# Attention and two MoE layers on one core: the last tokens' Q and K loaded with two heads exchanged in half of the batches

## The chip, the cores and the metric

The kernel runs on one core of a Trainium2 chip. A core has five engines that run their own instruction lists side by side: TensorE (PE) for matrix products, VectorE (DVE), ScalarE (ACT) and GpSimd (POOL) for elementwise work, and SyncE (SP), which here issues nearly all DMA transfers. They wait for each other and for landed transfers through semaphores. The metric is the device time of one execution in microseconds (us); lower is better.

## The reference, cut to what matters

Inputs are q, k and v of 8 batches, 8 heads, 576 tokens and 64 columns. Attention is within chunks of 64 tokens, so there are 9 chunks in each batch and head. Its output, read as 4608 tokens by 512 columns, goes through two feed-forward layers:

```python
scores = scale * np.matmul(q_c, k_c.transpose(0, 1, 2, 4, 3))   # per chunk of 64 tokens
attn = softmax(scores); out = np.matmul(attn, v_c)
x = out.transpose(0, 2, 1, 3).reshape(4608, 512)
y = (sigmoid(x @ w_gate) * (x @ w_val)) @ w_out                 # d_ff 1536
h = y @ w_in                                                    # d_ff 2048
g = np.where(h >= 1, h, np.where(h <= -1, 0, (h + 1)**2 / 4))
result = g @ w_out2
```

Weights come as 64-bit floats and all arithmetic is single precision.

## The kernel before, in words

**Stages.** The first, up to about 610 us, holds attention and the first layer's two projections; the rest of the span holds the other products, done by a seven-product (Strassen-like) scheme. Each full-precision product is three passes of rounded operands (lines 528 to 530 of `three`). PE is meant to be busy all through.

**Blocks.** The 4608 tokens are worked in nine blocks of 512. Eight are the first 512 tokens of one batch each. The block in the middle, number 4 (`REST`), collects the last 64 tokens of all eight batches: chunk c of that block is batch c. Each block has four pairs of heads (p = 0 to 3), with the two heads' 64 columns stacked on 128 partitions. While the projections of block b run (12 gate and 12 value columns of weights, 24 slots), the attention of a following block is done in between, one pair every six slots.

**One pair of heads.** `load` brings q and k (line 283 for block 4, line 312 for most others); a letter in `how` says in which layout, and "V", the default and block 4's, is transposed in 32 by 32 squares on DVE (line 336). `s` makes the scores: 16 products of 64 by 64 per pair (line 361; the trace counts two passes of each, x32). `m`, `e`, `n` and `w` make the softmax, `p` transposes the result on PE, `o` multiplies by v (line 422), `x` and `l` split the output into the projection's operands.

**Which part of PE a score product uses.** Its rows are the partitions its operands stand on (0 to 63 or 64 to 127), its columns the partitions it writes. Without exchange, head 0 always reads and writes the lower half and head 1 the upper. With `swap`, the second half of a block's tokens (u = 1) is loaded with the two heads' rows exchanged, so that there head 0 reads the upper partitions and writes the lower, and head 1 the reverse. `swap` holds for layouts V and S in every block but block 4.

**Order of the work.** The code is written out slot by slot: `at(slot, prio, ...)` sorts what is emitted between two projections, and each engine runs its instructions in that order. For blocks 3 and later, pair p of block b starts at slot 24(b-1)+6p-11. Its q is loaded two pairs earlier, its k one slot after that, its v 6.5 slots after its start, and `o` follows at 14. SP's one queue also carries, between these loads, the stores of finished projections (`gT<-sg`, line 845, four `sg` buffers), the raw weights of later layers (`raw`, lines 112 and 116) and the stores of their split forms (`swo`, `swi`, line 192). The program uses eight DMA semaphores in turn, so each issue also waits for the transfer eight places ahead of it.

Of the kernel before, what the change touches and what calls it, by code (L numbers as in the profile page):

```python
# [33 lines left out]
def kernel(  # L34
# [15 lines left out]
    nc = tc.nc  # L50
    P = 128
    B, H, S, D = q.shape
# [5 lines left out]
    BS = 512  # L58
# [176 lines left out]
    REST = NB // 2  # L235
    RS = S - BS

    def batch(blk):
        return blk - (blk > REST)
# [5 lines left out]
    class Whole:  # L245
# [14 lines left out]

        def swap(self, p):

            return self.b != REST and self.how[p] in "VS"

        def load(self, p, which=(0, 1)):
            t = self.alloc("qk") if 0 in which else self.raw[p]
            self.raw[p] = t
            how = self.how[p]
            if how == "V":

                t = t.rearrange("p i (t r) -> p i t r", r=32)
            elif how in "TS":

                t = t.rearrange("p i (j h d) -> p i j h d", h=2, d=D)
            else:
                t = t.rearrange("p i (h j d) -> p i h j d", h=2, d=D)
            for i in which:
                src = (q, k)[i]
                if self.b == REST:
                    for g in range(4):  # L280
                        h, j = divmod(g, 2)
                        for c in range(RS // 32):
                            nc.sync.dma_start(
                                out=t[32 * g:32 * g + 32, i, c::RS // 32],
                                in_=src[:, 2 * p + h, BS + 32 * c:BS + 32 * c + 32, 32 * j:32 * j + 32].rearrange(
                                    "b i r -> i b r"
                                ),
                            )
                else:
                    rows = src[batch(self.b), 2 * p:2 * p + 2, :BS]  # L290
                    if how == "M":
                        nc.sync.dma_start(
                            out=t[:, i].rearrange("i h j d -> i h (j d)"),
                            in_=rows.rearrange("h (i j) d -> i h (j d)", j=NC),
                        )
                    elif how in "TS":
                        n = 2 if self.swap(p) else 1
                        for u in range(n):
                            js = slice(u * NC // n, (u + 1) * NC // n)
                            for h in range(2):  # L300
                                nc.sync.dma_start(
                                    out=t[:, i, js, h],
                                    in_=rows[h ^ u].rearrange("(j i) d -> i j d", i=P)[:, js],
                                )
                    else:
                        n = 2 if self.swap(p) else 1
                        step = BS // n
                        for u in range(n):
                            for g in range(4):
                                h, j = divmod(g, 2)  # L310
                                part = rows[h ^ u, u * step:(u + 1) * step, 32 * j:32 * j + 32]
                                nc.sync.dma_start(
                                    out=t[32 * g:32 * g + 32, i, u * step // 32:(u + 1) * step // 32],
                                    in_=part.rearrange("(t i) r -> i t r", i=32),
                                )
            self.qk[p] = t
# [670 lines left out]
```

## Time and profile before

| | |
|---|---|
| median of 3 runs | 1638.9 us (1638.7 to 1639.31) |
| profiled execution | 1639.61 us, span 1637.8 us |
| PE busy | 1620.7 us, 99% of the span |
| DVE, ACT, POOL busy | 1081.2, 806.7, 360.0 us |
| DMA | 336.31 MB in 375733 packets, q1 busy 63.8% of 16 engines |
| issues on SP of q and k in layout V | 32 KB each |

The profile shows one execution. An engine's line number is that of the kernel; SPq is SP's sequencer, whose issue of a DMA has a duration of its own, and a transfer lands some us after its issue. The chain of waits follows the work that ended last back to the start; a line there says how long the end of the program hung on that piece.

### The profile page before, as it was taken

To read this page: it belongs to the slowest core of one execution; us is meant where nothing else is said; L and a number is where in the kernel's file an instruction comes from. 1 tells how busy PE (TensorE), PEld (TensorE's weight loads), DVE (VectorE), ACT (ScalarE), POOL (GpSimd) and SP (SyncE) were. 2 spreads that over 40 slices of the span, in tenths; PEclk is the share of its full clock that TensorE was granted. 3 is DMA by queue.
4 is the path that set the end of the run, shared out by engine and by line. 5 is a ranking of instruction groups with operands and counts; after the bars stand their busy time and mean duration, and the time that the engine had idled before them with its cause. 6 is when DMAs were issued, how large, how long until landed. Compare 5 with 4: busy or idle time off the path is not lost.

```text
span 1637.8 us, 27009 instructions
## 1 busy us (share of the span) xinstructions
PE 1620.7 (99%) x9764; PEld 1355.9 (83%) x9764; DVE 1081.2 (66%) x1944; ACT 806.7 (49%) x1374; POOL 360.0 (22%) x342
## 2 busy tenths in 40 slices
PE   7999999999999999999999999999999999999998
PEld 6777888888888888888988888889888888888888
DVE  6965554455455521488687766676766887878787
ACT  5764544455545431355455455445443545454544
POOL 2423444344444420000000164240420300000000
PEclk9999999999999999999999999999999999999999
DMA  8957877777778848352636744758659856445252
GB/s 205 269 131 193 236 230 207 206 211 237 223 224 231 264 159 322 138 170 89 218 125 236 269 181 177 289 222 312 237 221 402 337 173 174 140 118 187 71 144 37
DMA packets 375733, 336.31 MB, mean 205 GB/s; under 512 B 260432, under 2 KB 281936, under 8 KB 375600
## 3 DMA queue, kind: packets, MB, share of 16 engines
q1 hardware_dynamic: 375408, 334.39, 63.8%
q8 instruction: 77, 1.26, 0.3%
q14 instruction: 56, 0.46, 0.1%
q0 software_dynamic: 192, 0.20, 0.1%
HBM read 209.19 MB, written 125.30 MB: 204 GB/s over the span
## 4 chain that ended last, share of the span: by engine, by line
PE 95%; DVE 2%; DMA 1%; ACT 1%; SPq 1%; issue 0%; POOL 0%; POOLq 0%; DVEq 0%; ACTq 0%
PE P L528 19%; PE P L530 19%; PE P L529 19%; PE pr L528 11%; PE pr L530 11%; PE pr L529 11%; PE O L422 1%; PE S L361 1%; PE S L404 1%; DMA raw<-in_moe_w_gate_dram 1%; DMA gT<-sg 0%; DVE raw L135 0%; PE PT L404 0%; DMA qk<-in_q_dram 0%; DVE raw L127 0%
## 5 line engine op out<-in xcount | busy, mean ns | idle before, releaser
L528 PE MATMUL P<-op,w 128*128 128x512 f32 (+1 forms) x1540 | 567.3, 368 | 0.5 <-ACT R L616 0.5
L529 PE MATMUL P<-op,w 128*128 128x512 f32 (+1 forms) x1540 | 566.8, 368 | 0.0
L530 PE MATMUL P<-op,w 128*128 128x512 f32 (+1 forms) x1540 | 566.7, 368 | 0.0
L528 PE MATMUL pr<-x,w 128*128 128x512 f32 x864 | 341.7, 395 | 0.0
L530 PE MATMUL pr<-x,w 128*128 128x512 f32 x864 | 336.9, 390 | 0.0
L529 PE MATMUL pr<-x,w 128*128 128x512 f32 x864 | 336.6, 390 | 0.0
L528 PEld LDWEIGHTS P<-op,w 128*128 128x128 f32 x1540 | 290.5, 189 | 49.4 <-ACT R L616 1.3
L529 PEld LDWEIGHTS P<-op,w 128*128 128x128 f32 x1540 | 290.5, 189 | 48.0
L530 PEld LDWEIGHTS P<-op,w 128*128 128x128 f32 x1540 | 290.5, 189 | 47.9
L947 DVE TENSOR_TENSOR sg<-pr,sg 128x512 f32<-128x512 f32 x108 | 74.5, 690 | 300.2 <-PE pr L530 183.0
L595 ACT ACTIVATE op<-u 128x512 fp32r<-128x512 f32 (+1 forms) x280 | 158.7, 586 | 160.1 <-PE P L530 85.7
L618 DVE TENSOR_TENSOR R<-P,R 128x512 f32<-128x512 f32 (+1 forms) x180 | 114.5, 636 | 136.8 <-PE P L530 136.2
L601 DVE TENSOR_TENSOR op<-u,op 128x512 fp32r<-128x512 f32 (+1 forms) x272 | 168.4, 629 | 48.4 <-ACT op L595 45.5
L530 PEld LDWEIGHTS pr<-x,w 128*128 128x128 f32 x864 | 162.2, 188 | 34.4
L528 PEld LDWEIGHTS pr<-x,w 128*128 128x128 f32 x864 | 162.3, 188 | 33.1
L529 PEld LDWEIGHTS pr<-x,w 128*128 128x128 f32 x864 | 162.4, 188 | 32.1
L601 POOL TENSOR_TENSOR op<-y,op 128x512 fp32r<-128x512 f32 (+1 forms) x56 | 66.7, 1205 | 495.2 <-DMA w<-swi 334.5
L944 ACT ACTIVATE sg<-pr 128x512 f32<-128x512 f32 x108 | 64.4, 596 | 199.3 <-PE pr L530 197.5
L595 ACT ACTIVATE op<-in 128x512 fp32r<-128x512 f32 (+1 forms) x210 | 116.5, 585 | 91.9 <-DVE in L591 55.7
L747 ACT ACTIVATE ua<-ua,half 128x1024 f32<-128x1024 f32 (+1 forms) x80 | 82.9, 1060 | 132.2 <-DVE ua L726 131.6
L601 DVE TENSOR_TENSOR op<-in,op 128x512 fp32r<-128x512 f32 (+1 forms) x210 | 128.0, 637 | 22.8 <-ACT op L595 22.4
L616 ACT ACTIVATE R<-P 128x512 f32<-128x512 f32 (+1 forms) x198 | 105.3, 549 | 49.8 <-PE P L530 49.3
(69 smaller groups left out, 1452.4 us busy)
## 6 DMA issues: line engine op xcount, KB each, us to landing
w<-swi SPq DMA_DIRECT2D x84, 512.0 KB, 5.0
uT<-ua SPq DMA_DIRECT2D x64, 512.0 KB, 3.8
u<-uT SPq DMA_DIRECT2D x64, 512.0 KB, 6.2
gT<-sg SPq DMA_DIRECT2D x96, 256.0 KB, 3.9
in<-gT SPq DMA_DIRECT2D x48, 512.0 KB, 5.4
raw<-in_moe_w_out_dram SPq DMA_DIRECT2D x28, 512.0 KB, 5.5
w<-swp SPq DMA_DIRECT2D x28, 512.0 KB, 8.5
swi<-st SPq DMA_DIRECT2D x24, 512.0 KB, 3.9
```

The lines of the kernel that those rows point to most:

```text
L361: nc.tensor.matmul(banks[h ^ u][hs, c], lhsT=t[rows, 0, ts], rhs=t[rows, 1, ts], start=True, stop=True)
L404: nc.tensor.transpose(place, self.SP[p][0][:, c * P:(c + 1) * P], kv_["ident"])
L528: nc.tensor.matmul(o, lhsT=ah, rhs=bh, start=first, stop=False, skip_group_check=open_)
L529: nc.tensor.matmul(o, lhsT=ah, rhs=bl, start=False, stop=False, skip_group_check=open_)
L530: nc.tensor.matmul(o, lhsT=al, rhs=bh, start=False, stop=stop and last, skip_group_check=open_)
L595: nc.scalar.activation(o[:, 0], op_src(p, key), AF.Copy)
L601: eng.tensor_tensor(out=o[:, 1], in0=op_src(p, key), in1=f32(o[:, 0]), op=ALU.subtract)
L616: nc.scalar.activation(r(i), b, AF.Copy)
L618: nc.vector.tensor_tensor(out=r(i), in0=b, in1=r(i), op=ALU.add)
L747: nc.scalar.activation(u, u, AF.Square, scale=0.5, bias=half)
L944: nc.scalar.activation(sg, go, AF.Sigmoid)
L947: nc.vector.tensor_tensor(out=sg, in0=vo, in1=sg, op=ALU.mult)
```

## The change

`swap` now holds for block 4 too, and the loads of that block are cut in two: batches 0 to 3 (u = 0) come as before, batches 4 to 7 (u = 1) with the two heads' rows exchanged. For each of q and k and each pair, eight DMAs of 32 by 8 by 32 elements become sixteen of 32 by 4 by 32, with the same bytes in all. In `s`, which is not edited, line 360 then picks the other half of the partitions for u = 1.

```diff
--- before.py
+++ after.py
@@ -260,7 +260,7 @@
 
         def swap(self, p):
 
-            return self.b != REST and self.how[p] in "VS"
+            return self.how[p] in "VS"
 
         def load(self, p, which=(0, 1)):
             t = self.alloc("qk") if 0 in which else self.raw[p]
@@ -277,15 +277,17 @@
             for i in which:
                 src = (q, k)[i]
                 if self.b == REST:
-                    for g in range(4):
-                        h, j = divmod(g, 2)
-                        for c in range(RS // 32):
-                            nc.sync.dma_start(
-                                out=t[32 * g:32 * g + 32, i, c::RS // 32],
-                                in_=src[:, 2 * p + h, BS + 32 * c:BS + 32 * c + 32, 32 * j:32 * j + 32].rearrange(
-                                    "b i r -> i b r"
-                                ),
-                            )
+                    n = RS // 32
+                    for u in range(2):
+                        bs = slice(u * B // 2, (u + 1) * B // 2)
+                        for g in range(4):
+                            h, j = divmod(g, 2)
+                            for c in range(n):
+                                part = src[bs, 2 * p + (h ^ u), BS + 32 * c:BS + 32 * c + 32, 32 * j:32 * j + 32]
+                                nc.sync.dma_start(
+                                    out=t[32 * g:32 * g + 32, i, u * B // 2 * n + c:(u + 1) * B // 2 * n:n],
+                                    in_=part.rearrange("b i r -> i b r"),
+                                )
                 else:
                     rows = src[batch(self.b), 2 * p:2 * p + 2, :BS]
                     if how == "M":
```

Two places on SP's queue show it. The first is the load of pair 0 of block 4 (q, then k), between the stores of projections (`gT`), of split weights (`swo`) and a load of v (`vd`). Before:

```order
L329 DMA vd<-in_v_dram 128x4x64 x2
L283 DMA qk<-in_q_dram 32x8x32 x8
L192 DMA swo<-st 128x2x512 x2
L845 DMA gT_69<-sg 128x512
L283 DMA qk<-in_k_dram 32x8x32 x8
L192 DMA swo<-st 128x2x512
L845 DMA gT_69<-sg 128x512
```

After; a line number past the edit is higher by 2 or 4:

```order
L331 DMA vd<-in_v_dram 128x4x64 x2
L287 DMA qk<-in_q_dram 32x4x32 x16
L192 DMA swo<-st 128x2x512 x2
L847 DMA gT_69<-sg 128x512
L287 DMA qk<-in_k_dram 32x4x32 x16
L192 DMA swo<-st 128x2x512
L847 DMA gT_69<-sg 128x512
```

Each load has doubled its issues, and everything behind it stands behind eight more (q) or sixteen more (q and k) issues than before; nothing has changed places.

The second is the last of the four pairs, with the raw weights of the next layer (`raw`) and the v of block 4's pair 0 (`vd`, four issues) ahead of it. Before:

```order
L112 DMA raw<-in_moe_w_in_dram 128x4x128 x2
L324 DMA vd<-in_v_dram 64x4x64 x4
L283 DMA qk<-in_q_dram 32x8x32 x8
L845 DMA gT_69<-sg 128x512
L283 DMA qk<-in_k_dram 32x8x32 x8
L845 DMA gT_69<-sg 128x512
```

After:

```order
L112 DMA raw<-in_moe_w_in_dram 128x4x128 x2
L326 DMA vd<-in_v_dram 64x4x64 x4
L287 DMA qk<-in_q_dram 32x4x32 x16
L847 DMA gT_69<-sg 128x512
L287 DMA qk<-in_k_dram 32x4x32 x16
L847 DMA gT_69<-sg 128x512
```

Here 48 added issues of the three earlier pairs stand ahead of `vd`, and 64 ahead of what follows the last row.

## Rows read from the trace of the kernel before

**Rows 1.** The page: busy time of PE, its clock, the chain by engine.
```profile
PE 1620.7 (99%) x9764; PEld 1355.9 (83%) x9764; DVE 1081.2 (66%) x1944; ACT 806.7 (49%) x1374; POOL 360.0 (22%) x342
...
PEclk9999999999999999999999999999999999999999
...
PE 95%; DVE 2%; DMA 1%; ACT 1%; SPq 1%; issue 0%; POOL 0%; POOLq 0%; DVEq 0%; ACTq 0%
```

**Rows 2.** Chain of waits, 187 to 306 us: start us, us, what.
```profile
211.16 0.47 PE S L361 x32
...
229.19 0.93 PE S L361 x32
...
284.07 0.62 PE O L422 x32
284.70 0.93 PE S L361 x32
...
303.19 0.47 PE S L361 x32
```

**Rows 3.** Windows: length, busy PE, PEld, DVE, ACT, POOL, clock, DMA share, GB/s.
```profile
243.00:262.00 19.00, 19.00 (x143) 15.72 (x143) 9.65 (x20) 9.35 (x17) 8.73 (x9) 1.00 0.76 203
```

**Rows 4.** Timeline of SP, 186 to 266 us: start us, us, what.
```profile
186.72 5.59 SPq L283 DMA_DIRECT2D qk<-in_q_dram  x8
...
252.70 3.92 SPq L283 DMA_DIRECT2D qk<-in_k_dram  x8
...
261.76 3.39 SPq L324 DMA_DIRECT2D vd<-in_v_dram  x4
```

**Rows 5.** Line 283's DMA issues: min/median/max in ns, first and last start.
```profile
L283 SPq DMA_DIRECT2D qk<-in_q_dram x32: 311/450/2162, 186.7 to 251.7; - x32
L283 SPq DMA_DIRECT2D qk<-in_k_dram x32: 430/449/1166, 194.3 to 256.2; - x32
```

**Rows 6.** Line 845's DMA issues, 186 to 300 us, in the same columns.
```profile
L845 SPq DMA_DIRECT2D gT<-sg x18: 327/404/1343, 193.7 to 296.2; - x18
```

**Rows 7.** SP's waits, 186 to 262 us: total us, times, longest us.
```profile
SPq L283 <- DMA raw<-in_moe_w_in_dram: 2.1, 2, 1.8
SPq L324 <- PE pr L530: 1.1, 1, 1.1
SPq L845 <- DVE raw L135: 1.1, 1, 1.1
SPq L845 <- DVE raw L121: 0.9, 1, 0.9
SPq L845 <- DVE sg L947: 0.9, 2, 0.4
```

**Rows 8.** Line 324's DMA issues: ns of one, then us to landing.
```profile
L324 SPq DMA_DIRECT2D vd<-in_v_dram x16: 596/624/1766, 243.0 to 302.2; - x16
...
DMA to landing us min/median/max: 2.3/3.7/6.6
```

**Rows 9.** Tile vd, 500 to 506 us: issues in ns, then us to landing.
```profile
L329 SPq DMA_DIRECT2D vd<-in_v_dram x2: 413/458/502, 501.8 to 502.2; - x2
...
DMA to landing us min/median/max: 6.4/6.4/6.5
```

**Rows 10.** Chain of waits, 500 to 522 us: start us, us, what.
```profile
518.97 0.62 PE O L422 x32
```

**Rows 11.** Timeline of SP, 310 to 322 us.
```profile
314.04 1.03 SPq L112 DMA_DIRECT2D raw<-in_moe_w_in_dram  x2
```

**Rows 12.** Timeline of DVE, 312 to 322 us; in brackets the idle time before.
```profile
318.83 0.43 DVE L121 TENSOR_SCALAR raw<-raw 128x512 int32<-128x512 uint32 x1 [0.16 <-DMA raw<-in_moe_w_in_dram]
```

**Rows 13.** SP's waits, 560 to 600 us, the longest.
```profile
SPq L845 <- DVE sg L947: 15.1, 4, 5.0
```

**Rows 14.** Windows at the start, in the columns of rows 3.
```profile
10.00:15.00 5.00, 2.30 (x40) 1.85 (x40) 4.05 (x8) 3.19 (x6) 0.00 (x0) 1.00 0.91 204
15.00:20.00 5.00, 4.52 (x56) 4.16 (x57) 3.85 (x11) 2.77 (x7) 2.33 (x2) 0.66 1.06 250
```

## The prediction

> **What bounds the kernel now.** I read the page first. PE is busy for 99% of the span, 95% of the chain of waits runs over it, and its granted clock is nine tenths or more of the upper level (2.4 GHz) in every slice [rows 1]. In the stretch that holds block 4's loads nothing stands still on PE: 19.00 us busy of 19.00, clock 1.00 [rows 3]. So a product that gets shorter there shortens the program, as long as nothing else comes late.
>
> Next I read the chain around block 4, because it prices the edit's purpose directly. The scores of one pair take 0.47 us in the blocks before and after block 4, and 0.93 us in block 4 [rows 2]; there are four such pieces, at 229.19, 247.69, 266.20 and 284.70 us.
>
> Then SP, which no share of busy time on the page speaks of. Its timeline shows issue after issue: one load of q or k in block 4 is eight issues, 3.92 us where nothing held it up, and 5.59 us for the first, where something did [rows 4]. From 186 to 262 us its waits are few: the four largest for other engines are 1.1, 1.1, 0.9 and 0.9 us, 4.0 us of 76 us, and one of 2.1 us is for landings [rows 7]. An engine that issues without a pause is full, although the program never ended on it. That makes SP, not PE, the engine that this change is about.
>
> **The change part by part.** *Scores.* The four pieces of 0.93 us should become 0.47 us, since the second halves then use the other partitions as in the other blocks: 4 x 0.46 = 1.84 us less on PE [rows 2]. PE's instruction list is otherwise the same. The copies, the softmax and the products by v read the same tiles in the same order, so they cost what they did.
>
> *Loads.* 64 issues become 128, with the same bytes. Eight of today's take 3.92 us, 0.49 each, of which 0.45 is the issue itself [rows 5] and 0.04 the step to the next. The trace has no issue of 128 short runs. From above, a half-sized issue costs what the whole one does: 3.92 us more per load, 8 loads, 31.4 us. From below it costs the shortest issue on line 283, 0.311 us [rows 5], with the same 0.04: 16 x 0.351 = 5.6 us, 1.7 us more per load, 13.6 us in all. A gain is excluded, since an issue would have to fall under 0.245 us, half of today's step, and the shortest on this line is 0.311. The nearest row is the store of a projection, which has 128 runs too, though longer ones: 0.404 us at the median [rows 6]. I take it: 16 x 0.444 = 7.1 us, 3.2 us more per load, 25.5 us in all, between 187 and some 285 us.
>
> *What covers it.* SP could give up its 4.0 us of waiting for other engines. Beyond that it runs late, and everything on its queue behind the loads lands late: v, the projections' stores, raw weights, the q and k of later blocks. How late may they be? The v of block 4's second pair goes out at 261.76 us in four issues [rows 4]; the last starts near 264.5 us and lands a median 3.7 us later [rows 8], at 268.2 us, and the product that needs it starts at 284.07 us [rows 2]: 15.9 us of cover. Later it is less. A v issued at 502.2 us lands 6.5 us on, at 508.7 us [rows 9], for a product at 518.97 us [rows 10]: 10.3 us, the least that I found among the v loads. In blocks 5 to 8 every pair still brings sixteen issues for q and k, so SP has little with which to work off a delay before these loads end; only from 560 us on does it wait long for PE's results again (15.1 us for `sg` in 40 us) [rows 13]. So a delay of 25.5 us on SP, once built up, stays, and PE loses what the cover lacks: 25.5 - 15.9 = 9.6 us already at 284 us, and 25.5 - 10.3 = 15.2 us by 519 us. What PE loses it does not regain, being full to the end.
>
> The two sides that I leave out have opposite signs: SP's 4.0 us of waits, which would lessen the delay, and one load with no cover at all. The raw weights issued at 314.04 us are waited for at 318.83 us already (0.16 us) [rows 11, 12]; DVE runs in order, so its next projection's product stands behind that wait.
>
> The 1.84 us saved on PE do not come off: where v ends last, PE gets there 1.84 us sooner and waits 1.84 us longer. So the sum is 1639.61 + 15.2 = 1654.8 us for the profiled execution. That one stands 0.7 us above the median of the runs, so I forecast 1654 us for these.
>
> Here a rule of the Trainium skill speaks for the opposite. Its page "DMA: Bandwidth & Descriptors" (section "Issuing engines are not separate DMA queues") says that the time a sequencer needs to initiate a DMA is usually small relative to the DMA itself. By that rule the added issues hide, and the first rival below holds. This trace does not agree: eight issues take 3.92 us of a queue with next to no pause.
>
> **The rivals.** *First: the cover is enough.* The place is SP's queue between 187 us and 262 us, and the point is a delay below the 10.3 us of rows 9 and 10. With the lowest issue cost (13.6 us) and SP's 4.0 us of waits given up, the delay is 9.6 us, just under it. Then only the saving is left: 1639.61 - 1.84 - 0.7 = 1637.1 us, 0.11% below the median and not slower. For it speaks that PE has not waited for a v so far in this stretch; against it that both ends have to be taken at their best at once, and that the raw weights of rows 11 and 12 have no cover.
>
> *Second: no cover.* If the raw weights decide, or several in-order engines pass the delay on, PE loses nearly all: 25.5 us, or 31.4 us with the upper issue cost, 1664 to 1670 us. A clock that falls would add to it. After 5 us in which PE was busy for 2.30 us, the next 5 us had a granted clock of 0.66, part of them at the lower level (1.2 GHz) [rows 14]: 0.34 x 5 = 1.7 us lost each time, some 5 us for three such stalls. The Trainium skill, page "TensorE: Matmul & The Clock Gate" (section "Why this matters for your kernels"), warns of idle gaps between bursts of products for the same reason; the row at 15 us agrees, and no row shows it in the stretch of block 4.
>
> *Third: the scores stay at 0.93 us*, because something other than the partitions made block 4 slow. The loads would still end last, so the time is the forecast's; only with full cover does it show, as 1638.9 us. Block 4 is the only one of the later blocks without the exchange, which speaks against it.
>
> **How the numbers follow.** Forecast (SP late, part of it covered, PE 4 to 23 us later): 0.70. First rival: 0.12. Second: 0.15. Third: 0.03. What a measurement of this kernel can tell from no change is about 0.2%, 3.3 us. Faster by that is more than the whole saving of 1.84 us: 0.02. Within it: the first rival and the near end of the forecast, 0.10. Slower: 0.88. The range goes from 1640 us, the forecast's lower end with a delay barely over the cover, to 1668 us, inside the second rival; it leaves out the first rival and the second's far end, less than 2 in 10.
>
> **What the profile after would show.** The scores of block 4 at 0.47 us per pair: the saving is right. SP's loads of 16 issues: about 7.1 us each if the store is the right measure, 5.6 or 7.8 us at the ends. In 240 to 340 us PE should show idle time, put down to landings of v, to `sg` and to DVE behind raw weights, and SP's issues should come some 25 us later than now by 285 us. If PE is still full there and the program ends 1.8 us sooner, the cover was larger than I read. If PE's stalls sum to far more than 15 us, the cover was smaller, or the clock fell, which the windows would show.

## The result and the profile after

The changed kernel takes 1661.96 us (median of four runs, 1658.89 to 1662.75) against 1639.11 us for the kernel before. The ratio is 1.0137, with a 95% interval of 1.0125 to 1.0150: some 23 us slower. The profiled execution of the changed kernel is the lowest of its four, 1658.89 us with a span of 1657.1 us; before it was 1639.61 and 1637.8 us. The profiles therefore stand 19.3 us apart, and all that follows is worked out against these 19.3 us.

The page after, busy time of PE and the chain by engine, to be read against [rows 1]:

```profile
PE 1626.2 (98%) x9764; PEld 1357.6 (82%) x9764; DVE 1078.1 (65%) x1944; ACT 806.2 (49%) x1374; POOL 360.2 (22%) x342
...
PE 88%; SPq 4%; DMA 3%; DVE 2%; issue 1%; POOL 1%; ACT 1%; POOLq 0%; DVEq 0%; ACTq 0%
```

Two things add up. PE's idle time is the span less the busy time: 17.1 us before, 30.9 after, 13.8 more. And PE is busy 5.5 us longer, although four score pieces became shorter. The chain, which ran over SP's queue for 1% of the span, now does so for 4%.

SP's timeline after (start us, us, what), against [rows 4]:

```profile
276.98 7.57 SPq L287 DMA_DIRECT2D qk<-in_k_dram  x16
...
289.29 3.33 SPq L326 DMA_DIRECT2D vd<-in_v_dram  x4
```

The issues of the split loads, line 287 (min/median/max in ns, first and last start), and their landing, against [rows 5]:

```profile
L287 SPq DMA_DIRECT2D qk<-in_q_dram x64: 311/430/1481, 185.1 to 276.0; - x64
L287 SPq DMA_DIRECT2D qk<-in_k_dram x64: 426/430/1961, 196.5 to 284.1; - x64
...
DMA to landing us min/median/max: 1.5/1.8/5.2
```

An issue with half the bytes takes 0.430 us where the whole one took 0.449 or 0.450. A load that nothing holds up takes 7.57 us instead of 3.92: 3.65 us more, eight times 29.2 us. The v load that went out at 261.76 us before goes out at 289.29 us. Below, the start of this load less 261.76 us is called SP's lag; here it is 27.5 us.

What PE does meanwhile, by windows (length, then busy time of PE, PEld, DVE, ACT, POOL; clock, DMA share, GB/s), against [rows 3], where PE was full:

```profile
243.00:262.00 19.00, 17.60 (x138) 14.09 (x136) 7.16 (x13) 5.91 (x11) 7.80 (x8) 1.00 0.42 123
262.00:300.00 38.00, 30.23 (x230) 24.62 (x231) 12.71 (x26) 14.00 (x22) 10.19 (x11) 0.87 0.57 157
300.00:340.00 40.00, 35.28 (x256) 28.12 (x258) 19.82 (x41) 19.13 (x33) 15.29 (x17) 0.96 0.77 222
340.00:380.00 40.00, 39.68 (x323) 32.43 (x313) 19.83 (x40) 20.05 (x36) 17.71 (x19) 1.00 0.79 224
```

The second of these windows before:

```profile
262.00:300.00 38.00, 38.00 (x286) 31.48 (x285) 18.71 (x40) 19.90 (x33) 16.36 (x18) 1.00 0.71 198
```

All of the new idle time lies in these four, 1.40 + 7.77 + 4.72 + 0.32 = 14.2 us. In the first two DMA is less busy than before (0.42 and 0.57 of the engines' time, against 0.76 and 0.71), and a transfer of a split load lands 1.8 us after its issue where a whole one took 2.3 us, both at the median: the transfers don't crowd each other, they are handed out late. PE's waits from 180 to 600 us (us in total, times, longest):

```profile
PE O L424 <- DMA vd<-in_v_dram: 6.8, 5, 3.8
PE pr L530 <- ACT sg L946: 6.5, 2, 4.2
PE pr L530 <- DVE sg L949: 0.5, 1, 0.5
PE pr L531 <- DVE x L446: 0.3, 1, 0.3
```

There were none before. Half is v itself. The other half is nearly all `sg`, which ScalarE (ACT) writes. These are PE's two waits on ACT, and what ACT did just before each:

```profile
262.96 0.50 PE L530 MATMUL pr<-x,w 128*128 128x512 f32 x1 [2.29 <-ACT sg L946]
...
329.22 0.50 PE L530 MATMUL pr<-x,w 128*128 128x512 f32 x1 [4.22 <-ACT sg L946]
```

```profile
262.31 0.60 ACT L946 ACTIVATE sg<-pr 128x512 f32<-128x512 f32 x1 [7.62 <-DMA gT<-sg]
...
328.03 0.65 ACT L131 ACTIVATE raw<-raw 128x512 f32<-128x512 f32 x1 [13.77 <-DVE raw L127]
328.58 0.58 ACT L946 ACTIVATE sg<-pr 128x512 f32<-128x512 f32 x1
```

The first wait, 2.3 us, is for a store of the projections (`gT<-sg`): it frees the tile `sg`, and it stands on SP's queue behind the loads. The second, 4.2 us, is for the raw weights. ACT's `sg` comes after a piece of raw weights in its list, that piece waits for DVE, and DVE had just waited 12.2 us for the raw load:

```profile
326.84 0.43 DVE L121 TENSOR_SCALAR raw<-raw 128x512 int32<-128x512 uint32 x1 [12.19 <-DMA raw<-in_moe_w_in_dram]
```

The 0.5 us on DVE's `sg` at 304 us come after such a wait of DVE too (10.2 us). So PE stood 6.8 us for v, 2.3 us for a store and 4.7 us for raw weights, all of them on SP's one queue.

The granted clock of 0.87 from 262 to 300 us, part of that time at the lower level (1.2 GHz of 2.4), comes after such waits, and it shows in single pieces of PE's timeline (start us, us, what, idle before):

```profile
245.00 0.69 PE L424 MATMUL O<-spT,vd 64*64 64x64 f32 x32
...
269.80 1.44 PE L424 MATMUL O<-spT,vd 64*64 64x64 f32 x31 [3.83 <-DMA vd<-in_v_dram]
```

The same products take 0.69 us where PE had been busy, and 1.44 us after 3.83 us of standing still.

### The profile page after: what moved, and what is told of

Its sections match the earlier page's. It is cut to its first block, busy times and chain, and to the rows that moved or that the text cites. A ratio compares the mean times of both kernels' runs of the same rounds, so it can differ in the third digit from the quotient of the medians.

```text
span 1657.1 us, 27073 instructions
## 1 busy us (share of the span) xinstructions
PE 1626.2 (98%) x9764; PEld 1357.6 (82%) x9764; DVE 1078.1 (65%) x1944; ACT 806.2 (49%) x1374; POOL 360.2 (22%) x342
## 4 chain that ended last, share of the span: by engine, by line
PE 88%; SPq 4%; DMA 3%; DVE 2%; issue 1%; POOL 1%; ACT 1%; POOLq 0%; DVEq 0%; ACTq 0%
PE P L530 19%; PE P L531 19%; PE P L532 19%; PE pr L530 10%; PE pr L531 9%; PE pr L532 9%; DMA raw<-in_moe_w_in_dram 1%; SPq L287 1%; PE O L424 1%; PE S L363 1%; PE S L406 1%; POOL st L181 1%; SPq L303 1%; SPq L314 1%; SPq L192 0%
```

## The experiments

The theory: SP's queue is the bound in block 4; its lag passes to PE, less a cover. The rivals: the exchange itself costs; the smaller transfers load the DMA engines; the raw weights alone decide.

### Issues without the exchange, and the exchange without issues

```
e1_issues  (from after)
-            return self.how[p] in "VS"
+            return self.b != REST and self.how[p] in "VS"
-  part = src[bs, 2 * p + (h ^ u), ...
+  part = src[bs, 2 * p + h, ...
e2_out_side  (from before; block 4 alone, with cross(p): self.b == REST)
-  banks[h ^ u][hs, c], lhsT=t[rows, 0, ts], rhs=t[rows, 1, ts], ...
+  bank, out = (h, heads[h ^ u]) if self.cross(p) else (h ^ u, hs)
+  banks[bank][out, c], lhsT=t[rows, 0, ts], rhs=t[rows, 1, ts], ...
+  if self.cross(p):
+      at_ = h * BS // 2 + g % 2 * P + (h ^ g // 2) * CH
e3_out_side_all  (the same in every block; swap(p) returns False, so no load is split)
```

Expected of e1_issues: 

> After's split loads (16 issues each), but without the exchange: both halves keep their heads in place, so the scores of block 4 stay at 0.93 us as in before. Theory (SyncE's lag from 64 more issues is the whole loss): 1660 to 1664 us, the same vd waits on TensorE (about 6.8 us at the first late v), SyncE some 27 us behind before at 262 us. Rival (the loss comes with the exchange itself, for example from how the crossed scores and O pieces follow each other): about 1639 us, with no wait on vd.

Measured: 1659.64 us, ratio 1.0126 [1.0112, 1.0140], beside 1.0137 [1.0125, 1.0150] for the whole change. Its waits of PE, 180 to 600 us:

```profile
PE O L424 <- DMA vd<-in_v_dram: 6.9, 4, 4.2
PE pr L530 <- ACT sg L946: 5.5, 2, 3.7
```

The issues alone make the loss. The scores' 1.84 us, which this kernel lacks, is not seen: it is no slower than the whole change.

Expected of e2_out_side: 

> Before's loads word for word (8 issues each); the exchange is made where the scores of block 4 are written: the matmul of head h reads rows of h and writes partitions h^u of bank h, and the reads of the score tile follow. Theory (the exchange is worth 4 x 0.46 us and the issues alone cost): 1637.3 us, 1.8 below before, the four S pieces of block 4 at 0.47 us in the chain. Rival (the 0.46 us per pair comes back later as a wait, since the stretch behind is tied to loads): 1639 us. Second rival (writing across the halves is not concurrent): S stays 0.93, 1639 us.

Measured: 1636.59 us against 1638.88, ratio 0.9987 [0.9978, 0.9996]. The scores of block 4 in its chain of waits:

```profile
227.91 0.47 PE S L366 x32
...
245.95 0.47 PE S L366 x32
...
263.98 0.47 PE S L366 x32
...
282.01 0.47 PE S L366 x32
```

All four are at 0.47 us and PE never waits from 180 to 600 us. The gain of 2.3 us, 0.7 to 3.6 by the interval, holds the 1.84 us. So it doesn't matter whether the operands or the result change sides; one of the two has to.

Expected of e3_out_side_all: 

> The exchange on the output side in every block that has it, so no load is split any more, neither block 4's nor the second halves of the other blocks' loads. Theory: TensorE's share as in the kernel with it in block 4 alone, 1637.3 us; SyncE issues fewer DMAs throughout, and since before's blocks 0 to 3 and 5 to 8 have no TensorE wait worth more than a few us in sum, the gain beyond that is 0 to 2 us: 1635 to 1637.5. Rival (longer, undivided transfers land later and the first blocks wait for them): 1638 to 1642.

Measured: 1636.45 us, ratio 0.9985 [0.9976, 0.9994]. Fewer issues in the other blocks bring nothing that shows; PE had no wait on them from 185 to 800 us in the first place. It has the lowest median of all kernels here, and it can't be told from e2_out_side.

### The same issues on two queues

```
e4_pool  (from after)
-  nc.sync.dma_start(
+  (nc.gpsimd if u else nc.sync).dma_start(
```

Expected: 

> After, with the second half of each split load (64 of the 128 issues) given to GpSimd's queue, so that SyncE carries as many issues as in before. Theory (SyncE's issue time is the bound): SyncE's lag at 262 us goes to about 0, the waits on vd and raw go, 1637 to 1641 us if GpSimd takes its 64 issues beside its own work (at 1 us each 64 us, spread over 100 us). Rival (the smaller transfers load the DMA engines or queues): the waits on vd stay and the time is 1655 to 1665. If GpSimd itself comes late, waits on its tiles (sp, st) appear in TensorE's list instead.

Measured: 1637.18 us, ratio 0.9989 [0.9980, 0.9998], with the same 128 transfers of the same size as the changed kernel. The issues of the q loads on each engine, and PE in the window that was the worst:

```profile
L287 SPq DMA_DIRECT2D qk<-in_q_dram x32: 311/430/1456, 185.9 to 252.5; - x32
L287 POOL DMA_DIRECT2D qk<-in_q_dram x32: 548/551/777, 189.3 to 246.3; - x32
```

```profile
262.00:300.00 38.00, 38.00 (x307) 31.09 (x308) 20.06 (x42) 20.00 (x33) 16.86 (x18) 1.00 0.72 202
```

PE is full again. The size of the transfers costs nothing here; the serial issue on one queue does. GpSimd pays 0.551 us per issue, 35 us in all, and has them free.

### How much lag is covered: more and fewer issues

```
e8_one_pair, e5_two_pairs  (from after; P = 1 or 2)
-  return self.how[p] in "VS"
+  return self.how[p] in "VS" and (self.b != REST or p < P)
   (a load of a pair without the exchange is 8 issues, as in before)
e6_four  (from after: u in (0, 1) becomes z in (0, 1, 2, 3), u = z // 2)
+  bs = slice(z * B // 4, (z + 1) * B // 4)
```

Expected of e8_one_pair: 

> The exchange and the split loads in the first pair of block 4 alone: 16 issues more than before instead of 64, so a SyncE lag of 2 x 3.66 = 7.3 us by the measured step, and one score piece at 0.47 us (-0.46 us). Theory of the prediction (a cover of some 10 us before TensorE loses anything): 1638.5 us, no wait on vd. Rival (no cover, each us of lag is lost): 1646 us, with waits on vd or sg of some 7 us.

Measured: 1638.69 us, ratio 1.0001 [0.9991, 1.0010]. The v load, and PE:

```profile
268.01 3.38 SPq L327 DMA_DIRECT2D vd<-in_v_dram  x4
```

```profile
262.00:300.00 38.00, 38.00 (x286) 31.48 (x285) 17.87 (x37) 18.16 (x31) 16.87 (x18) 1.00 0.72 210
```

A lag of 6.25 us costs nothing: there is a cover, for the raw weights as well. DVE waited 21.8 us for raw loads between 180 and 420 us, and PE never waited for DVE.

Expected of e5_two_pairs: 

> The exchange and the split loads in the first two pairs of block 4: 32 issues more than before, a SyncE lag of 14.6 us by the measured step, two score pieces at 0.47 us (-0.92 us). Theory (a cover of 10 to 16 us, then one for one): 1638 to 1643 us. Rival (no cover): 1652 us. Rival (the loss goes by the number of issues in proportion, 24 us for 64): 1650 us.

Measured: 1646.68 us, ratio 1.0045 [1.0030, 1.0060], above the 1643 us that the theory allowed and below both rivals. The v load, and the two windows in which PE stands:

```profile
276.96 3.30 SPq L327 DMA_DIRECT2D vd<-in_v_dram  x4
```

```profile
243.00:262.00 19.00, 17.01 (x129) 13.95 (x128) 11.22 (x24) 9.66 (x16) 9.52 (x10) 0.91 0.86 250
...
300.00:340.00 40.00, 36.74 (x276) 29.50 (x275) 15.40 (x33) 14.25 (x27) 12.07 (x13) 0.96 0.73 195
```

Its waits of PE, 180 to 600 us, and what ACT did before the longest:

```profile
PE pr L531 <- ACT sg L947: 2.5, 1, 2.5
PE S L364 <- DVE qkT L339: 2.0, 1, 2.0
PE pr L532 <- DVE x L447: 0.7, 1, 0.7
```

```profile
315.54 0.67 ACT L131 ACTIVATE raw<-raw 128x512 f32<-128x512 f32 x1 [14.15 <-DVE raw L127]
316.12 0.57 ACT L947 ACTIVATE sg<-pr 128x512 f32<-128x512 f32 x1
```

With a lag of 15.2 us PE doesn't wait for v at all. The 2.5 us go back to the raw weights, by the same way as in the changed kernel (DVE had waited 11.9 us for the load). The 2.0 us are for a transpose on DVE that starts at 246.7 us, as a q load lands; DVE itself had come back at 242.2 us from a wait of 7.7 us for raw weights. Which of the two held it is open.

Expected of e6_four: 

> Each load of block 4 split in four (32 issues instead of 16, 128 more than after in all), the same rows and the same bytes. Theory (past the cover SyncE's lag passes to the end one for one, and an issue costs about 0.47 us whatever its size): 8 x 16 x 0.47 = 60 us over after, 1720 us, and some us more if the granted clock falls for longer. Rival (an issue costs by its bytes or rows, so half the size costs half): 1662 us. Between the two, 1690 us says that half of an issue's cost is fixed.

Measured: 1720.37 us, ratio 1.0497 [1.0479, 1.0514], as the theory had it. Busy time from the page, the issues of line 288, and the v load:

```profile
PE 1641.3 (95%) x9764; PEld 1367.4 (80%) x9764; DVE 1078.7 (63%) x1944; ACT 805.5 (47%) x1374; POOL 360.4 (21%) x342
```

```profile
L288 SPq DMA_DIRECT2D qk<-in_q_dram x128: 311/425/1911, 187.0 to 330.2; - x128
```

```profile
350.79 3.34 SPq L327 DMA_DIRECT2D vd<-in_v_dram  x4
```

Half the size again, and still 0.425 us per issue. Here is the lag beside the span over that of before (1637.8 us), both from the profiled executions:

```
kernel          issues added   SP's lag    span over before   lag less span
e8_one_pair          16         6.25 us        -1.6 us            (covered)
e5_two_pairs         32        15.2             7.2               8.0
the change           64        27.5            19.3               8.2
e1_issues            64        30.0            21.8               8.2
e6_four             192        89.0            81.2               7.8
```

In these kernels, whose queues differ in the number of issues and not in their order, each microsecond of lag past 8 us is one of span. Each row is one execution, and executions of one kernel differ too (1658.89 to 1662.75 us for the change). The slower clock doesn't come on top. In e6_four PE is 20.6 us longer busy than before (1641.3 against 1620.7), in the change 5.5, in e5_two_pairs 2.6 (1623.3), and the last column stays at 8. The reading is that where SP sets the pace, a product that runs slower takes the place of idle time.

### What stands behind SP

```
e7_raw_early  (from after)
-  (-1, w_load, a), (-1, w_load, b), ...
+  (-5, w_load, a), (-5, w_load, b), ...
e9_gT_pool  (from after, g_store, the stores of every block)
-  nc.sync.dma_start(out=dst[...], in_=sg)
+  nc.gpsimd.dma_start(out=dst[...], in_=sg)
e10_v_pool  (from after, both dma_start of v_load)
-  nc.sync.dma_start(
+  nc.gpsimd.dma_start(
```

Expected of e7_raw_early: 

> After, with the raw MoE weights that are prepared beside the attention loaded four slots earlier, so that this path, which has almost no cover, is taken off the lag. Theory A (TensorE loses by the v loads and by what is queued behind SyncE as a whole): 1657 to 1663 us, the waits on vd as in after. Theory B (the in-order engines stand behind VectorE's wait for raw, 35.2 us in after between 180 and 420 us, and hand it on to sg): the waits of VectorE on raw shrink, TensorE's 6.5 us on sg go, and the time falls to 1652 to 1656 us.

Measured: 1661.24 us, ratio 1.0138 [1.0123, 1.0153]. PE's largest waits, 180 to 600 us:

```profile
PE pr L530 <- ACT sg L946: 9.8, 2, 5.4
...
PE O L424 <- DMA vd<-in_v_dram: 1.4, 2, 0.7
```

The time is theory A's, but its list is not: the wait on v shrinks from 6.8 to 1.4 us, and that on `sg` grows from 6.5 to 9.8. DVE's waits for raw loads, 35.2 us in the changed kernel between 180 and 420 us, are gone from its list, and both waits on `sg` now go back to stores. The first of them:

```profile
270.34 0.60 ACT L946 ACTIVATE sg<-pr 128x512 f32<-128x512 f32 x1 [11.17 <-DMA gT<-sg]
```

The edit also did something that was not meant, as SP's timeline shows:

```profile
192.36 9.09 SPq L287 DMA_DIRECT2D qk<-in_q_dram  x16
...
295.96 3.77 SPq L326 DMA_DIRECT2D vd<-in_v_dram  x4
```

SP comes to block 4's first load 7.2 us later than in the changed kernel (185.1 us), and the lag at the v load is 34.2 us. The span is 1658.5 us, 20.7 us over before. So 13.5 us of lag are covered here instead of 8: taking the raw weights out of the way widened the cover by about as much as the lag grew. The run doesn't clear the raw weights; that they set the 8 us fits it, but with two things changed at once it is not shown.

Expected of e9_gT_pool: 

> After, with the projections' stores (gT<-sg, 13 issues between 186 and 300 us on SyncE) given to GpSimd's queue. SyncE is freed of 13 x 0.49 = 6.4 us there, so its lag of 27.5 us goes to 21. So far the span was SyncE's lag less 8 us (lag 15.2, 27.5 and 89.0 us; span 7.2, 19.3 and 81.2 us over before). Theory A (the 8 us hold whatever is queued on SyncE): 21 - 8 = 13 us over before, 1652 us. Theory B (it was the late stores, for whose sg tile ScalarE and then TensorE waited, that had only 8 us; v has 10 to 16 us): 5 to 11 us over before, 1644 to 1650 us, and TensorE's waits on sg go. Rival C (GpSimd, in order, stands behind VectorE for each store and delays its own work): 1658 us or more.

Measured: 1649.11 us, ratio 1.0066 [1.0048, 1.0084]. The v load and PE's waits:

```profile
282.15 3.05 SPq L326 DMA_DIRECT2D vd<-in_v_dram  x4
```

```profile
PE O L424 <- DMA vd<-in_v_dram: 4.7, 3, 3.1
PE pr L530 <- ACT sg L946: 1.8, 1, 1.8
```

The lag is 20.4 us, near the 21 worked out. The span is 1646.6 us, 8.8 over before, so the cover is 11.6 us instead of 8, inside theory B's range. The wait on `sg` does not go, though, it falls from 6.5 to 1.8 us. What is left of it is not the stores':

```profile
318.42 0.68 ACT L131 ACTIVATE raw<-raw 128x512 f32<-128x512 f32 x1 [11.76 <-DVE raw L127]
...
319.64 0.50 PE L530 MATMUL pr<-x,w 128*128 128x512 f32 x1 [1.83 <-ACT sg L946]
```

It is the raw weights again. The stores' own part is gone, and some 3.5 us more of the lag are covered; but the interval of the ratio, 1646.5 to 1652.4 us, still touches theory A's 1652. Which of the stores, v and the raw weights has the least cover is not settled.

Expected of e10_v_pool: 

> After, with the v loads (10 to 14 issues of some 0.62 us on SyncE between 185 and 290 us) given to GpSimd's queue, so that v is no longer behind the split loads and SyncE is freed of 6 to 9 us. Theory A (span = lag - 8 us for all that is left on SyncE): lag 19 to 21 us, 1650 to 1652 us. Theory B (v alone decides): 1637 to 1641 us, no wait of TensorE on anything. Theory B' (the stores decide, v did not): as A, with waits on sg in TensorE's list and none on vd. Rival C (GpSimd holds up): 1658 us or more.

Measured: 1683.35 us, ratio 1.0276 [1.0257, 1.0295]. The first 60 us of its trace:

```profile
0.00:60.00 60.00, 30.29 (x393) 25.59 (x394) 23.50 (x56) 22.93 (x38) 16.15 (x22) 0.77 0.62 168
```

Before, PE was busy for 49.44 us of these 60. The edit moves the v loads of every block, and those at the start stand in GpSimd's list ahead of its pieces of the softmax (`sp`). PE's longest wait in these 60 us:

```profile
PE PT L406 <- POOL sp L394: 19.5, 1, 19.5
```

That is rival C, long before block 4 is reached, so the run answers nothing about block 4. What the lag of v alone is worth stays open.

## Why the prediction was right

*The scores: right.* 0.47 us with the exchange on either side. The first of the four pieces in the chain of the changed kernel (start us, us, what), at 229.19 us with 0.93 in [rows 2]:

```profile
227.66 0.47 PE S L363 x32
```

*That the 1.84 us would not come off: right,* e1_issues without them is as slow as the change.

*The cost of an issue: the right kind, sized a little low.* The store of [rows 6] gave 0.404 us; it was 0.430, and the load 7.57 us instead of 7.1. From eight loads that is 29.2 us, not 25.5. The lag came to 27.5 because in this execution SP reached block 4's first load 1.6 us earlier than in the one before (185.1 us against 186.7); its waits in the stretch sum to 7.3 us in both, so it gave up none of them.

*The cover: the step that was mis-sized.* I took 10.3 us from a v load at 502 us [rows 9, 10] and found 8 us. The first half of this step held: I had put PE's loss at 9.6 us by the product at 284 us, and when PE reached that product, at 292.8 us, it had stood 8.2 us, with 0.9 us still to come. The second half did not. No product waited for v after 295 us, so that 10.3 us came near 8 us is luck. I looked at v alone; the stores (2.3 us of PE's waits) and the raw weights (4.7 us) stood on the same queue, and PE's waits after 300 us, which end the loss, go back to the raw weights. With the stores on another queue the cover was 11.6 us. With the 8.0 us of e5_two_pairs the sum is 27.5 - 8.0 = 19.5 us, against a difference of the spans of 19.3 us; mine was 25.5 - 10.3 = 15.2 us.

*The raw weights without cover [rows 11, 12]: wrong for a short lag, right for a long one.* A lag of 6.25 us passed without a loss: that DVE just reached its load in time didn't mean that someone waited for DVE. At 15.2 and 27.5 us PE did wait, by the way that I had named (DVE in order, a projection's product behind it) and through ACT besides. I had left this side out of the sum; it is 4.7 us of PE's waits.

*The clock on top: wrong in the second rival.* The granted clock fell to 0.87 from 262 to 300 us, as the row at 15 us suggested [rows 14]. But the span followed the lag in the four kernels above whatever their clock, so it must not be added.

*The rivals.* Cover enough: it was for one pair (6.25 us), not for four. No cover: excluded by the same kernel, though its in-order engines passed the delay on past 8 us. Scores that stay at 0.93 us: excluded by the 0.47 us. 1661.96 us lies 8 us above the forecast, between it and the second rival's 1664: 4.1 us of it are the two terms, and 3.1 us come from the other runs of the changed kernel being slower than the profiled one (1658.89 against a median of 1661.96), which no trace here explains; the rest is the 0.7 us that I took off for the median, which went the other way.

*The rule on issuing engines.* The Trainium skill, page "DMA: Bandwidth & Descriptors" (section "Issuing engines are not separate DMA queues"), says that issuing on several engines saves only the sequencers' time, usually small relative to the DMA. The first half agrees with e4_pool, which gained just that. The second holds for one transfer, 0.430 us of issue against a landing of 1.8 us, but not for the queue: landings ran side by side here and issues one after another, and 64 more of them made a lag of 27.5 us.

## What to carry to other kernels

Count the issues of a queue before splitting a load: in this kernel an issue cost nearly the same with 32, 16 or 8 KB, and a queue that issues without a pause is full, whatever the page's shares say. The cover of such a queue is the least slack of all that stands on it, stores that free a tile included, so read each customer and not only the load next to the change. Follow a wait past the engine that it is put down to: the same `sg` of ACT was late for a store in one place and for raw weights in another. A side can be exchanged where a product is written as well as where its operands are loaded, and the former needs no DMA.

## What was not expected of the hardware

An issue on SP took 0.450, 0.430 and 0.425 us for 32, 16 and 8 KB: it has next to nothing to do with the bytes. On GpSimd it took 0.551 us, and 64 of them beside its work cost no time. Products after a standstill of 3.83 us took 1.44 instead of 0.69 us, and the granted clock of the 1.5 us from 269.80 us on was 0.50, the lower level. Some 22 us of longer busy time in e6_four (20.6 us and the 1.84 us saved) left the span where the queue had put it.
